# One written order for every operation from the first load to the third MLP round, with each attention period ordered on its own

## The chip, the cores and the metric

The kernel runs on one core of one Trainium2 chip. The metric is the device time of one execution in microseconds; lower is better. A core has a matrix engine (TensorE, PE in the rows; its weight loads are PEld), a vector engine (DVE), a scalar engine (ACT), GpSimd (POOL) and a queue that issues transfers (SP). Each engine works through its own list of instructions in order, and waits on semaphores for the others.

## What is computed

Three layers follow one another (batch 2, 8 heads, 768 positions, head size 64, width 512):

```python
mask = q_bucket[:, :, :, None] == k_bucket[:, :, None, :]     # buckets: signs of q, k times a 64 x 6 projection
scores = np.where(mask, scale * np.matmul(q, k.transpose(0, 1, 3, 2)), -1e9)
attn = softmax(scores); x = attn @ v                           # attention
theta = x @ w_theta                                            # mixing layer
y = w_tok_r @ (x * cos(theta)) + w_tok_i @ (x * sin(theta))
u = x + y; x = u + relu(u @ w_ch)
xn = layernorm(x) * g_ln; out = x + relu(xn @ w_ch1) @ w_ch2   # MLP
```

Every matrix product is done as three products of a high and a low part of its operands, so each operand is split first ("hi", a rounding cast, and "lo", the difference).

## The kernel before

**Attention.** The 16 heads of 768 rows are cut into 48 periods of 256 rows (two tiles of 128). Head h has periods 3h to 3h+2. For period p and tile i the operations, by the names of the order's text, are: `S.p.i` four PE matmuls of the scores into PSUM (`s_mm`, L332), `M.p.i` the row maximum on DVE (L340), `E.p.i` the exponential on ACT (L356), `R2.p` the reciprocal of the row sums on DVE (L363), `tb.p` a small POOL operation (L347), `n.p.i` the normalisation on POOL (L367), `U.p.u` four PE transposes into one PSUM bank (u = 0, 1, 2; L380; `U.p.0` and half of `U.p.1` read `n.p.0`, the rest `n.p.1`), `H.p.u` and `L.p.u` the hi and lo part of the transposed weights on ACT (L389) and DVE (L101), `PV.p` twelve PE matmuls with v (L405), `O.p` on ACT (L414) and `X.p` on DVE (L423), which empty the one PSUM bank of `PV`. So `PV.p+1` cannot start before `X.p`.

**Operands of a head.** The query and key of a head are stacked by six transfers inside SBUF (`sk.h`, L248 to L253) and two small ones for the bucket bits (`sb.h`, L262 and L263). A period's second pair of score matmuls reads the bits. The bits are made from the split q and k by `bits_chunk` on PE, one operation each on ACT (L304) and DVE (L310), and a last one on POOL (`bw`, L666, for pairs 1 to 3; `B1` to `B4` for pairs 4 to 7).

**Side work in the attention.** The weights of theta (eight tiles) are converted while the attention runs: one POOL, one ACT, two DVE operations (`conv_low` L125 and `conv_join` L131), one ACT, one POOL. There are also the splits of v, q and k and the first splits of x (`z_hi`, `z_lo`).

**What sets the order.** The program is emitted operation by operation, and each engine runs its own in that order. Periods 0 to 7 are written out, one token per operation, in a text `head`. From step 8 on a fixed row of tokens with a lag (`plan`) is repeated for each step, and another (`plan_b`) for the four steps that make the bits of the last pairs; the side work hangs on three slots of the plan ("G", "C", "D") by step numbers. The lines that matter:

```python
    plan = (
        ("Sa", 0), ("U0", 2), ("L2", 3), ("nb", 2), ("Ma", 0), ("H0", 2), ("X", 4), ("D", 0),
        ("R2", 1), ("U1", 2), ("Sb", 0), ("Mb", 0), ("H1", 2), ("U2", 2), ("Ea", 0), ("ta", 0), ("H2", 2),
        ("G", 0), ("na", 1), ("PV", 3), ("tb", 0), ("Eb", 0), ("L0", 2), ("C", 0), ("L1", 2), ("O", 3),
    )
```

From the end of the attention on, texts again name every operation: `tail` (the last periods beside the first theta products `z_m`, L790), `half1` (mixing and channel layer), `trans` (the first three MLP rounds). Later MLP rounds follow two fixed texts.

Of the kernel before, what the change touches and what calls it, by code (L numbers as in the profile page):

```python
# [33 lines left out]
def attn_moe_kernel(  # L34
# [398 lines left out]
    def theta_steps(c, x, y):  # L433

        r = slice(256 * x, 256 * x + 256)
        o = {}

        def s():
# [3 lines left out]
            o["t"] = conv_tiles(ap_, th_st[c, x])  # L442
            conv_s(*o["t"])

        return (
            (at, 0, s), (at2, y, lambda: conv_y(*o["t"])), (at3, 1, lambda: conv_low(*o["t"])),
            (at3, 1 + y, lambda: conv_join(*o["t"])), (at2, 1 + y, lambda: cast(act, WA["h"][:, c, r], o["t"][1])),
            (at, 2 + y, lambda: sub(pool, WA["l"][:, c, r], o["t"][1], WA["h"][:, c, r])),
        )
# [104 lines left out]
    TS = tuple(range(22, 46, 3))  # L554
    bg, bg2, bg3 = {}, {}, {}

    def at(step, fn, *args):
        bg.setdefault(step, []).append((fn, args))

    def at2(step, fn, *args):  # L560
        bg2.setdefault(step, []).append((fn, args))

    def at3(step, fn, *args):
        bg3.setdefault(step, []).append((fn, args))


    for h in range(5, B * H):
        at({8: 20}.get(h, 3 * h - 7), stack_dma, h)
        at({8: 21, 9: 21}.get(h, 3 * h - 7), stack_bits, h)
    v_steps = {2: (6, 9, 10), 3: (15, 16, 18), 4: (20, 22, 23)}  # L570
    for n in range(2, NPAIR):
        ld, *hi = v_steps.get(n, (6 * n - 6, 6 * n - 3, 6 * n - 2))
        at(ld, load_v, n)
        for x in range(2):
            at2(hi[x], v_hi, n, act, x)
            at(hi[x] + 1, v_lo, n, pool, x)
    for n, ld in ((6, 8), (7, 13)):
        at(ld, load_raw, n)
    for nm, n, *hi in (
        ("k", 5, 7, 11), ("q", 5, 8, 9), ("k", 6, 12, 13), ("k", 7, 14, 15),  # L580
        ("q", 6, 16, 17), ("q", 7, 17, 18),
    ):
        for x in range(2):
            at2(hi[x], split_hi, nm, n, act, x)
            at(hi[x] + 1, split_lo, nm, n, pool, x)
    for i in range(8):
        c, x = divmod(i, 2)
        at(TS[i] - 2 if i < 2 else max(TS[i] - 3, TS[i - 2] + 2), theta_load, c, x)
        for slot, d, fn in theta_steps(c, x, int(i < 7)):
            slot(TS[i] + d, fn)  # L590
# [18 lines left out]
    for step, fn, j, a in (  # L609
        (30, z_hi, 0, 0), (31, z_hi, 0, 1), (32, z_lo, 0, 0), (32, z_lo, 0, 1),  # L610
        (33, z_hi, 1, 0), (36, z_hi, 1, 1), (37, z_lo, 1, 0), (38, z_lo, 1, 1),
        (38, z_hi, 2, 0), (39, z_hi, 2, 1), (43, z_lo, 2, 0), (44, z_lo, 2, 1),
    ):
        at(step, fn, j, a)
# [3 lines left out]

    def run_bg(q):
        def run(p):  # L620
            for fn, args in q.pop(p, []):
                fn(*args)
        return run

    ops = {
        "Sa": lambda p: s_mm(p, 0), "Sb": lambda p: s_mm(p, 1),
        "Ma": lambda p: s_max(p, 0), "Mb": lambda p: s_max(p, 1),
        "ta": lambda p: None, "tb": s_lone,
        "Ea": lambda p: s_exp(p, 0), "Eb": lambda p: s_exp(p, 1),
        "R2": s_recip, "na": lambda p: s_norm(p, 0), "nb": lambda p: s_norm(p, 1),  # L630
        "B1": lambda p: bits_chunk(*bq[p], "T1"), "B2": lambda p: bits_y_(*bq[p]),
        "B3": lambda p: bits_b_(*bq[p]), "B4": lambda p: bits_p_(*bq[p]),
        "PV": pv_mm, "O": pv_evac_a, "X": pv_evac_b,
    }
    for u in range(3):
        ops[f"U{u}"] = lambda p, u=u: p_transpose(p, u)
        ops[f"H{u}"] = lambda p, u=u: p_hi(p, u)
        ops[f"L{u}"] = lambda p, u=u: p_lo(p, u)
    K0 = 8
    nxt = {op: K0 - d for op, d in plan}  # L640

# [45 lines left out]
    head = """
        sh.k.0.0.0 pb.0.0 pb.0.2 sl.k.0.0.0 pb.0.1 sh.k.0.1.0 sl.k.0.1.0 sh.q.0.0.0 sl.q.0.0.0 sh.q.0.1.0 ac.0
        sl.q.0.1.0 fk ac.1 ay.0 ay.1 kz.1.1 ac.2 ay.2 D.0.0 ab.0 lr.3.0 ab.1 ac.3 sh.k.1.2.0 D.0.1 ay.3 ab.2
        sh.q.1.2.0 aw.0.1 aw.1.1 pb.1.0 aw.2.0 kz.0.0 ab.3 Q.0.0 M.0.0 Q.0.1 warm.17 pb.1.2 E.0.0 lr.3.1 M.0.1  # L690
        sl.q.1.2.1 E.0.1 pb.1.1 D.1.0 sl.k.1.2.0 sh.k.3.2.0 Q.1.0 tb.0 lr.2.0 R2.0 lr.2.1 aw.3.0 M.1.0 n.0.1
        sk.1 sh.k.2.2.0 D.1.1 n.0.0 E.1.0 U.0.2 Q.1.1 U.0.0 sh.q.3.2.0 sl.k.2.2.0 sl.k.3.2.0 U.0.1 sl.q.3.2.1
        H.0.0 D.2.0 M.1.1 H.0.2 bc.0.1 L.0.2 L.0.0 Q.2.0 sh.q.2.2.0 E.1.1 M.2.0 by.0 tb.1 H.0.1 bc.1.0 D.2.1
        lv.0 bb.0 sl.q.2.2.1 L.0.1 by.1 sb.1 R2.1 Q.2.1 bw.0.1 n.1.0 E.2.0 bb.1 vh.0.0 lr.4.0 bc.3.1 M.2.1
        vh.0.1 S.3.0 lr.5.0 vl.0.0.0 bc.2.0 by.3 bw.1.1 E.2.1 U.1.0 by.2 M.3.0 S.3.1 bb.3 n.1.1 U.1.1 E.3.0
        vl.0.1.1 R2.2 bb.2 U.1.2 tb.2 bw.3.1 H.1.0 M.3.1 n.2.0 H.1.1 S.4.0 PV.0 H.1.2 E.3.1 L.1.0 L.1.1 lr.4.1
# [787 lines left out]
```

## Time and profile before

| what | value |
|---|---|
| time, median of 3 runs | 664.09 us (663.68 to 665.66) |
| span of the profiled execution | 662.6 us, 11210 instructions |
| the three runs against that span | 1.0 to 3.0 us above it |
| PE busy | 99% of the span |
| DVE, ACT, POOL busy | 84%, 63%, 47% |
| granted TensorE clock | 1.00 throughout |

The span runs from the first to the last instruction of the profiled execution; the profile does not list that execution's own time, so the runs' distance to the span stands for what lies around it. A busy share of PE does not tell its pace: matmuls overlap, and the record of one ends some 0.16 us after the next could start, so that a short wait of PE shows as a longer step from one start to the next.

### The profile page before, as it was taken

The page shows a single profiled execution, that of the slowest core. Times are in us where ns is not written, and L with a number is a line of the kernel's source. Part 1 is how long each engine was busy: PE and PEld are TensorE (multiplying, and loading weights), DVE is VectorE, ACT ScalarE, POOL GpSimd, SP SyncE. Part 2 cuts the span into 40 slices and gives each one's busy share as a digit, 9 for nine tenths or more (in the row PEclk, how much of TensorE's full clock was granted, in tenths as well). Part 3 has the DMA queues.
Part 4 walks back from the last instruction along what each step waited for, and adds up shares of the span by engine and source line. Part 5 has one row for each costly group of instructions (what it writes and reads, how often), then busy time and mean ns, then how long its engine had stood idle before and what let it go on. Part 6 is the DMA issues. An engine that isn't in the chain of part 4 may idle for free.

```text
span 662.6 us, 11210 instructions
## 1 busy us (share of the span) xinstructions
PE 657.1 (99%) x3771; PEld 591.7 (89%) x3771; DVE 557.5 (84%) x1002; ACT 416.4 (63%) x864; POOL 310.5 (47%) x418
## 2 busy tenths in 40 slices
PE   9999999999999999999999999999999999999998
PEld 7999999999999888888888888989998999999997
...
GB/s 248 240 176 173 135 108 114 116 172 128 127 96 0 161 51 61 80 75 95 148 81 64 48 96 65 63 1 64 64 65 66 62 96 33 97 49 46 1 80 111
DMA packets 32374, 62.24 MB, mean 94 GB/s; under 512 B 4482, under 2 KB 11732, under 8 KB 32317
## 3 DMA queue, kind: packets, MB, share of 16 engines
...
q8 instruction: 30, 0.49, 0.3%
q14 instruction: 27, 0.22, 0.1%
...
## 4 chain that ended last, share of the span: by engine, by line
PE 95%; DVE 2%; DMA 1%; SPq 1%; POOL 1%; issue 0%; ACT 0%; POOLq 0%
PE o L1191 20%; PE acc L856 15%; PE o L405 9%; PE s L332 9%; PE t L380 9%; PE Z L1148 8%; PE a L898 5%; PE v L1148 5%; PE th L790 4%; PE zy L1148 2%; PE Y L1148 2%; PE bits L286 2%; PE s L503 1%; PE xt L967 1%; PE ut L883 1%; DMA tk<-bits 1%
## 5 line engine op out<-in xcount | busy, mean ns | idle before, releaser
L1191 PE MATMUL o<-arena,hh 128*128 128x512 f32 (+1 forms) x388 | 119.1, 388 | 0.0
L367 POOL TENSOR_SCALAR pn<-p,l,M 128x768 f32<-128x768 f32 x96 | 94.6, 986 | 38.8 <-DVE l L363 25.6
L340 DVE TENSOR_REDUCE M<-s 128x1 f32<-128x772 f32 x96 | 90.9, 947 | 4.1 <-PE s L515 2.0
L101 DVE TENSOR_TENSOR ptl<-t,pth 128x512 fp32r<-128x512 f32 x144 | 90.6, 678 | 1.3 <-ACT pth L389 1.0
L356 ACT ACTIVATE p<-s,M 128x772 f32<-128x772 f32 x96 | 87.5, 912 | 2.4 <-DVE M L340 2.0
L117 POOL TENSOR_SCALAR cs<-st 128x512 f32<-128x512 f32 (+2 forms) x68 | 44.8, 665 | 84.6 <-DVE cy L131 75.1
L1191 PEld LDWEIGHTS o<-arena,hh 128*128 128x128 f32 x388 | 72.1, 188 | 13.6
L389 ACT ACTIVATE pth<-t 128x512 fp32r<-128x512 f32 x144 | 81.1, 599 | 4.3 <-PE t L380 3.0
L332 PE MATMUL s<-tk,tq 128*128 128x386 f32 (+1 forms) x360 | 82.8, 351 | 0.0
L380 PE MATMUL t<-ident,pn 128*128 128x128 f32 x576 | 80.3, 273 | 0.4 <-POOL pn L367 0.4
L1191 PE MATMUL o<-arena,hl 128*128 128x512 f32 (+1 forms) x194 | 75.5, 389 | 0.0
L856 PE MATMUL acc<-arena,tokh 128*128 128x512 f32 x240 | 75.3, 395 | 0.0
L380 PEld LDWEIGHTS t<-ident,pn 128*128 128x128 f32 x576 | 68.5, 141 | 6.3 <-POOL pn L367 1.4
L1156 ACT ACTIVATE sn<-Z 128x384 f32<-128x384 f32 x39 | 19.2, 492 | 67.2 <-PE Z L1148 67.2
L332 PEld LDWEIGHTS s<-tk,tq 128*128 128x128 f32 (+1 forms) x360 | 59.4, 190 | 0.1
L856 PEld LDWEIGHTS acc<-arena,tokh 128*128 128x128 f32 x240 | 44.0, 188 | 8.5
L1198 DVE TENSOR_TENSOR U<-o,U 128x512 f32<-128x512 f32 x48 | 32.9, 689 | 21.2 <-PE o L1191 20.5
L856 PE MATMUL acc<-arena,tokl 128*128 128x512 f32 x120 | 46.9, 391 | 0.0
L405 PE MATMUL o<-pth,vv 128*128 128x256 f32 x288 | 46.0, 295 | 0.1
L131 DVE SCALAR_TENSOR_TENSOR cy<-cy,cs 128x512 uint32<-128x512 uint32 (+2 forms) x72 | 41.4, 575 | 3.6
L114 ACT ACTIVATE cy<-st 128x512 f32<-128x512 f32 (+2 forms) x72 | 39.5, 561 | 7.8 <-DVE tokl L101 2.5
L125 DVE SCALAR_TENSOR_TENSOR cs<-st,cs 128x512 uint32<-128x512 uint32 (+2 forms) x76 | 44.1, 580 | 0.2
(260 smaller groups left out, 1481.8 us busy)
## 6 DMA issues: line engine op xcount, KB each, us to landing
...
```

Of the source, the lines that this page charges most:

```text
L101: eng.tensor_tensor(out=o, in0=i, in1=f(hi), op=ALU.subtract)
L117: eng.tensor_scalar(out=s, in0=f(t)[:, :, 1], scalar1=0.0, scalar2=1.0, op0=ALU.mult, op1=ALU.mult)
L332: pe.matmul(ps[:, hf, 0:HW], lt[0:K, x * 128:(x + 1) * 128], rt[0:K, hf, :], start=(K == 128), stop=(K != 128),)
L340: vec.tensor_reduce(out=m_t[p][:, 0, i:i + 1], in_=s_ps[p, i][:, :, 0:HW], axis=AX.XY, op=ALU.max, negate=True)
L356: act.activation(pt, ps[:, :, 0:HW], AF.Exp, bias=m[:, 0, i:i + 1], accum_out=l_t[p][:, 0, i:i + 1])
L367: pool.tensor_scalar(out=pn.rearrange("p (h c) s -> p h (c s)", h=2), in0=p_t.pop((p, i))[:, :, 0:HALF], scalar1=l_t[p][:, 1, i:i + 1], sc ...
L380: pe.transpose(ps[:, w * 128:(w + 1) * 128], pn_t[p, i][:, c, :], ident)
L389: act.activation(ph, t_ps[p, u], AF.Copy)
L405: pe.matmul(ps, vv[:, c, e].rearrange("p a d -> p (a d)"), x[:, c::NI, :], start=(k == 0), stop=(k == 2 * NI - 1),)
L856: pe.matmul(acc, w[:, x, t * 128:(t + 1) * 128], z[:, x, y, :], start=(j == 0 and k == 0), stop=(j == NI - 1 and k == 5),)
L1148: pe.matmul(ps_t[r, b], W1[g][y][:, w, d, :], XB[s][x][:, z, d, :], start=(first == 1 and k == 0), stop=(k == 5), skip_group_check=True,)
L1191: pe.matmul(ps, lt[:, i * 128:(i + 1) * 128], W2[g][:, y, x, n], start=(k == 0), stop=(k == 5))
```

## The change

`plan`, `plan_b` and the slots are removed. `head` now names every operation of all 48 periods and of the side work, in one text; `tail`, `half1` and `trans` are written anew. The 2175 operations are the same ones, with the same engines; only their order differs, and 38 periods from 8 to 45 have 38 different orders. Cut to its core:

```diff
-    plan = (
-        ("Sa", 0), ("U0", 2), ("L2", 3), ("nb", 2), ("Ma", 0), ("H0", 2), ("X", 4), ("D", 0),
...
+    def theta_step(c, x, k):
...
+        elif k == 2:
+            conv_low(*t)
+        elif k == 3:
+            conv_join(*t)
...
     head = """
-        sh.k.0.0.0 pb.0.0 pb.0.2 sl.k.0.0.0 pb.0.1 sh.k.0.1.0 sl.k.0.1.0 sh.q.0.0.0 sl.q.0.0.0 sh.q.0.1.0 ac.0
...
+        sh.k.0.0.0 sh.k.0.1.0 pb.0.0 pb.0.2 sh.q.0.0.0 sh.q.0.1.0 fk sl.k.0.0.0 pb.0.1 sl.k.0.1.0 sl.q.0.0.0 ac.0
...
-    steps = [(k, plan_b if k - 2 in bq else plan) for k in range(K0, NPER)]
...
+    run(head)
```

**Place 1: a middle period on PE and POOL** (the stretch from `S.32.0` to `PV.29`). Names are those above: s is S, t is U, o is PV, pn is n; the first number is the period, the second the tile or the third u. PE before:

```order
L332 MATMUL s32_0_2528<-tk10_2066,tq10_2064 128x386 x2
L332 MATMUL s32_0_2528<-tk210_2067,tq210_2065 128x386 x2
L380 MATMUL t30_0_2533<-ident_62,pn30_0_2505 128x128 x4
L380 MATMUL t30_1_2548<-ident_62,pn30_0_2505 128x128 x2
L380 MATMUL t30_1_2548<-ident_62,pn30_1_2539 128x128 x2
L332 MATMUL s32_1_2553<-tk10_2066,tq10_2064 128x386 x2
L332 MATMUL s32_1_2553<-tk210_2067,tq210_2065 128x386 x2
L380 MATMUL t30_2_2560<-ident_62,pn30_1_2539 128x128 x4
L405 MATMUL o29_2575<-pth29_2465,vv4_2018 128x256 x6
```

PE now:

```order
L332 MATMUL s32_0_2527<-tk10_1960,tq10_1958 128x386 x2
L332 MATMUL s32_0_2527<-tk210_1961,tq210_1959 128x386 x2
L380 MATMUL t30_0_2540<-ident_62,pn30_0_2519 128x128 x4
L380 MATMUL t30_1_2546<-ident_62,pn30_0_2519 128x128 x2
L380 MATMUL t30_1_2546<-ident_62,pn30_1_2497 128x128 x2
L380 MATMUL t30_2_2551<-ident_62,pn30_1_2497 128x128 x4
L332 MATMUL s32_1_2562<-tk10_1960,tq10_1958 128x386 x2
L332 MATMUL s32_1_2562<-tk210_1961,tq210_1959 128x386 x2
L405 MATMUL o29_2583<-pth29_2487,vv4_1853 128x256 x6
```

POOL before, around the two normalisations of period 30:

```order
L367 TENSOR_SCALAR pn30_0_2505<-p30_0_2418,l30_2417,M_66 128x768
L347 TENSOR_SCALAR M_66<-M_66 128x2
L367 TENSOR_SCALAR pn30_1_2539<-p30_1_2444,l30_2417,M_66 128x768
L98 TENSOR_SCALAR xhl0_2571<-xT0_486 128x256
L367 TENSOR_SCALAR pn31_0_2573<-p31_0_2489,l31_2488,M_66 128x768
```

POOL now:

```order
L367 TENSOR_SCALAR pn30_1_2497<-p30_1_2462,l30_2439,M_66 128x768
L367 TENSOR_SCALAR pn30_0_2519<-p30_0_2440,l30_2439,M_66 128x768
L347 TENSOR_SCALAR M_66<-M_66 128x2
L101 TENSOR_TENSOR vv5_2312<-vs5_2125,vv5_2312 128x6x64
L367 TENSOR_SCALAR pn31_1_2581<-p31_1_2537,l31_2523,M_66 128x768
```

`U.30.2` has moved ahead of `S.32.1`. Both normalisations of a period now stand in a row, tile 1 first, and in the whole text both come ahead of the period's `U.p.0`; in the plan `n.p.1` came after `U.p.0`, in the next step.

**Place 2: the theta operations on DVE** (same stretch; cs and cy are the theta tiles, l is R2, xT is X). Before:

```order
L340 TENSOR_REDUCE M_66<-s32_0_2528 128x1
L423 TENSOR_TENSOR xT1_2255<-o28_2507,ot28_2526 64x256
L131 SCALAR_TENSOR_TENSOR cy_2423<-cy_2423,cs_2424 128x256
L363 RECIPROCAL l31_2488<-l31_2488 128x2
L340 TENSOR_REDUCE M_66<-s32_1_2553 128x1
```

Now:

```order
L340 TENSOR_REDUCE M_66<-s32_0_2527 128x1
L423 TENSOR_TENSOR xT1_2279<-o28_2506,ot28_2534 64x256
L125 SCALAR_TENSOR_TENSOR cs_2320<-st_2138,cs_2320 128x256
L363 RECIPROCAL l31_2523<-l31_2523 128x2
L131 SCALAR_TENSOR_TENSOR cy_2319<-cy_2319,cs_2320 128x256
L340 TENSOR_REDUCE M_66<-s32_1_2562 128x1
```

In the plan the sixteen stand always between X and R2, in periods 25, 26, 28, 29, 31, 32, 34, 35, 37, 38, 40, 41, 43, 44 and twice in 46. Now their place and period vary: 23, 25, 26, 29, twice 32, 35, 36, twice 38, 40, 42, 43, 46 and twice 47; in period 32 one stands ahead of R2 and one behind it.

**Place 3: the transfer queue (SP) in the first periods** (tk2h, tq2h: the second operand pair of head h; the rows with bits are `sb.h`). Before:

```order
L253 DMA tk22_518<-lok1_85 64x772
L174 DMA vs1_533<-in_v_dram 128x6x128
L166 DMA raws_76<-in_qT_dram 128x768
L262 DMA tk22_518<-bits_312 7x772
L263 DMA tq22_516<-bits_312 7x2x384
L248 DMA tq4_601<-hiq2_94 64x768
```

Now:

```order
L253 DMA tk24_384<-lok2_93 64x772
L106 DMA st_465<-in_w_theta_dram 128x512
L174 DMA vs1_490<-in_v_dram 128x6x128
L262 DMA tk24_384<-bits_340 7x772
L263 DMA tq24_382<-bits_340 7x2x384
L262 DMA tk22_329<-bits_340 7x772
L263 DMA tq22_327<-bits_340 7x2x384
```

The stack of head 4 and both its bit transfers have moved ahead of the bit transfers of head 2, which period 6 needs first.

## Rows read from the trace of the kernel before

**Rows 1.** The page's first lines: span, then busy time, share, instructions.

```profile
span 662.6 us, 11210 instructions
...
PE   657.1 (99%) x3771; PEld 591.7 (89%) x3771; DVE 557.5 (84%) x1002; ACT 416.4 (63%) x864; POOL 310.5 (47%) x418
```

**Rows 2.** Waits of PE's weight loads, whole span: us in total, times, longest.

```profile
PEld t L380 <- POOL pn L367: 1.4, 5, 0.6
...
PEld o L405 <- DVE xT L423: 0.9, 4, 0.3
PEld xps L773 <- PE xps L773: 0.6, 1, 0.6
PEld zy L1148 <- DVE c L1163: 0.5, 1, 0.5
...
PEld xps L773 <- DVE r L806: 0.3, 1, 0.3
```

**Rows 3.** PV matmuls, stretch 53 to 86 us: count, durations, first and last start.

```profile
L405 PE MATMUL o<-pth,vv x48: 278/282/365, 53.2 to 83.1; 128*128 128x256 f32 x48
```

**Rows 4.** The same, stretch 125 to 224 us.

```profile
L405 PE MATMUL o<-pth,vv x138: 277/282/387, 126.3 to 221.3; 128*128 128x256 f32 x138
```

**Rows 5.** PE in order of time, 156 to 165 us: start, us, instructions merged.

```profile
156.21 0.97 PE L405 MATMUL o<-pth,vv 128*128 128x256 f32 x6
...
160.71 0.97 PE L405 MATMUL o<-pth,vv 128*128 128x256 f32 x6
...
162.94 1.04 PE L380 MATMUL t<-ident,pn 128*128 128x128 f32 x8
```

**Rows 6.** DVE in order of time, same stretch.

```profile
160.23 0.42 DVE L423 TENSOR_TENSOR xT<-o,ot 64x256 f32<-64x256 f32 x1
160.68 0.17 DVE L363 RECIPROCAL l<-l 128x2 f32<-128x2 f32 x1
160.77 0.94 DVE L340 TENSOR_REDUCE M<-s 128x1 f32<-128x772 f32 x1
161.62 1.87 DVE L101 TENSOR_TENSOR ptl<-t,pth 128x512 fp32r<-128x512 f32 x3
163.42 0.95 DVE L340 TENSOR_REDUCE M<-s 128x1 f32<-128x772 f32 x1
164.29 0.40 DVE L423 TENSOR_TENSOR xT<-o,ot 64x256 f32<-64x256 f32 x1
164.62 0.40 DVE L125 SCALAR_TENSOR_TENSOR cs<-st,cs 128x256 uint32<-128x256 uint32 x1
164.95 0.15 DVE L363 RECIPROCAL l<-l 128x2 f32<-128x2 f32 x1
```

**Rows 7.** POOL in order of time, same stretch.

```profile
161.05 0.99 POOL L367 TENSOR_SCALAR pn<-p,l,M 128x768 f32<-128x768 f32 x1 [0.35 <-DVE l L363]
162.12 0.22 POOL L347 TENSOR_SCALAR M<-M 128x2 f32<-128x2 f32 x1
```

**Rows 8.** POOL and DVE in order of time, at 40 us.

```profile
40.02 0.62 POOL L347 TENSOR_SCALAR M<-M 128x2 f32<-128x2 f32 x1
...
40.01 0.54 DVE L221 SCALAR_TENSOR_TENSOR lok<-raws,hik 128x384 fp32r<-128x384 f32 x1
```

**Rows 9.** ACT and PE in order of time, first 9 us.

```profile
4.55 0.52 ACT L210 ACTIVATE hik<-raws 128x384 fp32r<-128x384 f32 x1 [0.65 <-DMA raws<-in_kT_dram]
...
5.37 0.44 PE L286 MATMUL bits<-hik,pb_hi 128*128 128x384 f32 x1
```

**Rows 10.** POOL, SP and PE in order of time, 31 to 37 us.

```profile
31.76 0.66 POOL L666 TENSOR_SCALAR bits<-bb,cst_sb 64x384 fp32r<-64x384 f32 x1
...
32.44 0.84 SPq L263 DMA_DIRECT2D tq<-bits  x1
...
36.50 0.96 PE L332 MATMUL s<-tk,tq 128*128 128x386 f32 x4
```

More of the change, by code (lines that the diff above doesn't have):

```diff
@@ L441, in s @@
                 WA["l"] = const.tile([128, 4, 512], F32R, tag="wAl", name="thl")
[L442 to L449, printed above, removed]
-    order.enter_context(tc.manual_schedule())
-    plan = (
[3 rows of a table removed]
-    )
-    plan_b = (
[4 rows of a table removed]
-    )
+            th_o[c, x] = conv_tiles(ap_, th_st[c, x])
+        t = th_o[c, x]
+        if k == 0:
+            conv_s(*t)
+        elif k == 1:
+            conv_y(*t)
+        elif k == 2:
+            conv_low(*t)
+        elif k == 3:
+            conv_join(*t)
+        elif k == 4:
+            cast(act, WA["h"][:, c, r], t[1])
+        else:
+            sub(pool, WA["l"][:, c, r], t[1], WA["h"][:, c, r])
+    order.enter_context(tc.manual_schedule())
     PH = "kq"
@@ L553, in attn_moe_kernel @@
         pool.memset(f(t[64:128]), 0.0)
[L554 to L590, printed above, removed]
     zx, zq_ = {}, {}
@@ L607, in z_lo @@
         sub(pool, z_slot(j, a, 1), z_src(j, a), z_slot(j, a, 0))
[L609 to L614, printed above, removed]
     bq = {}
@@ L617, in attn_moe_kernel @@
         bq[17 + x] = ([4, 5, 6, 7], PH[x // 2], x % 2)
[L619 to L640, printed above, removed]
     def stk_bits(h):
@@ L654, in g_load, with raw_pair @@
         sp.dma_start(out=gT, in_=g_ln.rearrange("(c p) -> p c", p=128))
+    def raw_pair(n):
+        load_raw(n)
     def kz_copy(y, e):
@@ L690, in attn_moe_kernel @@
[L690 to L694, printed above, removed]
@@ L700, in attn_moe_kernel @@
-        n.4.0 L.3.0 vh.1.0 L.3.2 PV.2 E.5.1 L.3.1 sl.q.4.0.1 U.4.2 O.2 vh.1.1 M.6.0 sk.3 R2.5 X.2 vl.1.0.1
-        U.4.0 sb.3 S.6.1 tb.5 H.4.0 sl.k.4.1.0 sb.4 U.4.1 H.4.2 M.6.1 n.5.0 E.6.0 H.4.1 L.4.0 E.6.1 PV.3 n.5.1
-        S.7.0 U.5.0 sh.q.4.1.0 O.3 L.4.2 L.4.1 M.7.0 H.5.0 U.5.2 S.7.1 X.3 R2.6 tb.6 U.5.1 E.7.0 H.5.1 H.5.2
-        M.7.1 PV.4 vl.1.1.1 L.5.0 sl.q.4.1.1 n.6.0 E.7.1 tb.7 O.4 L.5.1
-    """
-    for w in head.split():
-        op, *args = w.split(".")
-        hops[op](*(int(x) if x.isdigit() else x for x in args))
@@ L710, in attn_moe_kernel @@
-    steps = [(k, plan_b if k - 2 in bq else plan) for k in range(K0, NPER)]
-    for k, now in steps:
-        for op, d in now:
-            if op == "G":
-                run_bg(bg)(k - 2)
-            elif op == "C":
-                run_bg(bg2)(k - 2)
-            elif op == "D":
-                run_bg(bg3)(k - 2)
-            elif op[0] == "B":
-                ops[op](k - 2)
-            else:
-                while nxt[op] <= min(k - d, NPER - 1):
-                    ops[op](nxt[op])
-                    nxt[op] += 1
+        sh.k.0.0.0 sh.k.0.1.0 pb.0.0 pb.0.2 sh.q.0.0.0 sh.q.0.1.0 fk sl.k.0.0.0 pb.0.1 sl.k.0.1.0 sl.q.0.0.0 ac.0
@@ L727, in attn_moe_kernel, with run @@
+        tq.3.1.5 O.44 E.47.1 tb.47
+    """
+    def run(text, **names):
+        for w in text.format(**names).split():
+            op, *args = w.split(".")
+            ops[op](*(int(x) if x.isdigit() else x for x in args))
+    run(head)
     bctx.close()
@@ L1333, in attn_moe_kernel @@
+        xb_l.0.1.4.1 madd.1.0.1 xb_h.0.1.5 ch_at.6 cv_h.e.1 xb_l.0.1.5.0 mix.35.0 cv_y.e.2 cv_l.e.1.1 madd.1.1.1
+        ch_ah.6 ch_al.6 mix.35.1 cv_b.e.2 xb_l.0.1.3.0 ch_at.9 cv_h.e.2 xb_h.0.1.2 cv_l.e.2.1 xb_l.0.1.2.0
     """
@@ L1377, in attn_moe_kernel @@
+        xb_h.1.1.3 xb_l.1.1.4.1 o_mm.1.3 h_hi.2.11 xb_l.1.1.3.0 xb_h.1.1.5 xb_l.1.1.5.1 prod.2.5 o_add.1.3 prod.2.7
+        o_mm.1.5 snap.2.3 h_add.2.22 h_lo.2.11 h_hi.2.22 prod.2.4 h_lo.2.22 o_add.1.5 prod.2.3 h_hi.2.21 h_lo.2.21
+        o_add.1.4
     """
```

325 lines of the change are left out of this document (166 added, 159 removed), and 6 rows, old and new, of tables (plan, plan_b).

## The prediction

> **What bounds the kernel now.** I read the page first. PE is busy 657.1 us of a span of 662.6 [rows 1], so no other engine's total can set the end; but the busy share hides short waits, since the record of a matmul reaches past the start of the next. The second view is therefore the table of waits for PE's weight loads [rows 2], where a late operand shows, and the third the pace of PE: how far the starts of the same block lie apart.
>
> The waits first. Away from the start, five groups are worth naming: the transposes waited five times for the normalisation on POOL (1.4 us, the longest 0.6), PV four times for X on DVE, which empties its one bank (0.9), and the transposes of x and a product of the MLP waited 0.6, 0.3 and 0.5 [rows 2]. The first two lie in the part that the repeated plan orders (from 53 us on); the last three, 1.4 us together, lie in `tail` and `trans`, where every operation already had a written place.
>
> The pace second. From 53 to 86 us there are 48 PV matmuls with the hi part, six for each period, so eight periods; the sixth of a block starts 0.69 us after the first (the six last 0.97 [rows 5], one lasts 0.28 [rows 3]). The first starts at 53.2, the last at 83.1, so seven steps are 29.9 - 0.69 = 29.2 us and a period is 4.17 us [rows 3]. No PE wait of the table falls in them, so 4.17 is what PE's own work takes. From 126.3 to 221.3 there are 138, hence 23 blocks and 22 steps: (95.0 - 0.69) / 22 = 4.286 us [rows 4]. Where the theta weights are converted, a period is thus 0.115 us longer, together 2.5 us. With the single wait of 0.6 us, which lies between the two stretches, the plan's part loses **3.1 us**. All that the change could remove is these 3.1 and the 1.4 of the texts: 4.5 us of 662.6.
>
> Why theta costs there: DVE. One period of it, from R2 to R2, is 160.68 to 164.95 [rows 6]: R2 0.09, M 0.85, three L 1.80, M 0.87, X 0.33, the theta operation 0.33. Without theta that is 3.94 us of the 4.17 that PE needs, so 0.23 us are left in a period, less than one theta operation. The plan puts 16 of them into 22 periods: 16 x 0.33 / 22 = 0.24 us a period against 0.23. DVE falls behind and X comes late: at 160.71 PV starts as X, begun at 160.23 and 0.42 long, ends, and it comes 4.50 us after the PV before it (156.21) instead of 4.17 [rows 5, 6].
>
> **The change, part by part.**
> - *Work.* The operations and their engines are the same. A gain can come only from waits of PE.
> - *Theta on DVE (place 2).* 14 of the 16 operations now lie in the 24 periods from 23 to 46, that is 14 x 0.33 / 24 = 0.19 us a period, below the 0.23; two moved into the last period, beside the theta products. The load alone no longer forces a wait. But they still come in twos (32 and 38 have two each), so some of them should still reach PE: two in one period make DVE 0.66 - 0.23 = 0.43 us late. Bounds for what remains of the plan's 3.1 us: below, nothing, as in the periods up to 53 us, which were written out singly and have the same operations and none of these waits; above, the density of the other written texts, 1.4 us in about 260 us (24 to 53 us and 220 to 450), times the 168 us from 53 to 221: 0.9 us. I take 0.5: the work is that of the former, but DVE is as full as nowhere in it. **Gain 3.1 - 0.5 = 2.6 us.** The wait of 0.6 for POOL was one long hold-up in one period, and goes with the plan.
> - *PE's order within a period (place 1).* `U.p.2` ahead of `S.p+2.1` issues the same matmuls; PE's pace by itself does not change. It gives H.2 and L.2 more time before PV. Counted as nothing; what covers it is that the four score matmuls that moved behind are needed by M, and DVE is busy with three L by then.
> - *Both normalisations ahead of `U.p.0`.* A deadline that comes earlier for the second of them; its price is a rival below. In the sum: nothing.
> - *Tail, half1, trans.* Rewritten, as they were written before: the same density of waits, so 1.4 us before and 1.4 us now. The ends are 0 and twice as much.
> - *The first microseconds.* ACT now splits the second half of k, which waits for its transfer until 4.55 and takes 0.52 [rows 9], ahead of the two casts of the projection. These end at about 5.4 instead of before 4, and the difference made from them on DVE at about 5.6; the first bits matmul started at 5.37 [rows 9]. The four bits products now stand together, ahead of both score groups, so part of the delay may be won back. Bounds 0 and 0.4 us; I take **a loss of 0.2**.
> - *SP (place 3).* Head 2's bits are now issued behind the stack of head 4, a theta tile, v and head 4's bits. The last q bits on POOL ended at 32.42 and the transfer that reads them was issued at 32.44 for 0.84; `S.6.0` started at 36.50 [rows 10]. In the new POOL order some 1.6 us of other work stands ahead of the last bits, so about 34.0, then three small transfers at 0.84 each: issued by 36.5. `S.6.0` itself now stands behind `PV.2` and starts 1.4 us later, about 38, its second pair 0.36 after. The cover is the landing time of the last transfer, which no row gives; if it takes 2 us the operand is just in time. Bounds 0 and 0.5; I take 0.
>
> Sum: -2.6 + 0.2 = -2.4 us. Against the span this is 662.6 - 2.4 = 660.2; against the median of the runs, 664.09 - 2.4 = **661.7 us**, since the runs lie 1.0 to 3.0 above the span and nothing outside the span changes.
>
> **A rule weighed.** The small POOL operation M took 0.62 us where it ran beside a DVE operation that reads two SBUF operands, and 0.22 us in a stretch without one [rows 7, 8]. The Trainium skill, "GPSIMD Engine Reference", § 8 Key points, says that GpSimd shares its SBUF interfaces with VectorE and contends with its instructions in a 2-port mode or with two SBUF inputs; by this rule the trace agrees, with the 0.40 us. The theta operations read two SBUF operands. In the plan they stood ahead of R2, and the normalisation waits for R2, so they never ran beside it; in the new order four of them (periods 32, 36, 38 and 43) stand right behind R2 and run beside `n`. If each holds it up by 0.40 us and nothing absorbs it, 1.6 us come back: 663.3 us. That is the first rival.
>
> **Rivals.**
> - *Contention of theta and n*: 661.7 + 1.6 = 663.3, by the paragraph above. Against it: four places of forty periods, and `n` has some slack where R2 is early. Chance 0.10.
> - *The waits only move.* The theta operations stay in the same stretch and in twos, DVE keeps over 95% of PE's period, and the written texts themselves have 1.4 us of waits, so a written order is no proof of none. If the plan's 3.1 us stay, the start takes its 0.2: 664.3. Chance 0.16.
> - *All of it goes*: 664.09 - 4.5 = 659.6. For it: the load on DVE falls below the limit, and the periods up to 53 us show that such an order can run without waits. Against: two of the three written texts have some. Chance 0.19.
> - *Slower: the second normalisation comes too late for `U.p.0`.* In a period delayed by theta R2 starts at 160.68, `n` at 161.05, and it lasts 0.99 [rows 6, 7]; the next transposes start at 162.94 [rows 5], with one `n` done and the second needed only later. Now both must be done: 0.37 + 2 x 0.98 + about 0.1 to hand over = 2.43 us after R2, and there are 162.94 - 160.68 = 2.26. If R2 stays that late in all 40 periods, each waits 0.17 us: 6.8 us lost, while the old 3.1 us go (the waiting gives DVE its time): 664.09 + 3.7 = 667.8. It decides at R2 later than 2.43 us before the transposes. Against it: where DVE is not behind, R2 is up to 0.23 us earlier, and in several of the new periods R2 stands ahead of X or of M. Chance 0.13.
>
> **How the numbers follow.** The forecast has 0.42, with a spread of its own from 660.4 (nothing left at the plan, no loss at the start, 0.6 less in the texts) to 662.8 (0.9 left, 0.4 and 0.5 lost at the start and the bits). About 0.3%, 2.0 us, is what a measurement of this kernel tells from no change, so faster means below 662.1 and slower above 666.1. Of the forecast 0.30 lies below 662.1 and 0.12 above. Faster: 0.30 + 0.19 = 0.49. Same: 0.12 + 0.10 + 0.16 = 0.38. Slower: 0.13. The range from 659.4 to 664.8 holds all but the slow case and a little of the edges.
>
> **What would show it.** Right: PV starts 4.17 to 4.2 us apart from 126 to 221 us where they were 4.286, X and `pn` gone or below 0.6 us together in the table of waits, the first bits matmul at 5.4 to 5.8. Wrong: waits of transposes for `pn` spread over many periods (the slow rival), POOL's `pn` longer beside theta (contention), the score matmuls of period 6 waiting for their bits, or new waits after 220 us above 1.4.

## The result: slower by 0.9%

| | before | after |
|---|---|---|
| time, median | 664.4 us (663.5 to 665.9, 6 runs) | 670.7 us (668.8 to 673.5, 6 runs) |
| ratio | 1 | 1.0094, 95% interval 1.0073 to 1.0115 |
| span of the profiled execution | 662.6 us | 670.1 us |

The kernel is 6.3 us slower where 2.4 us less were forecast; the range ended at 664.8. The profiled execution took 671.84 us, 1.8 above its span. Three of the six runs have a granted clock of 0.999 or 1.000 and take 668.8 to 669.9 us, the other three 0.995 to 0.997 and 671.6 to 673.5; the profiled one is among the latter. The page of the profile after, first lines and the row of the clock:

```profile
span 670.1 us, 11172 instructions
...
PE 661.1 (99%) x3771; PEld 594.0 (89%) x3771; DVE 559.9 (84%) x1002; ACT 414.2 (62%) x864; POOL 310.5 (46%) x418
...
PEclk8999999999999999999999998999999999999999
```

Busy times answer to [rows 1] within a few us: the work is the same, and 7.5 us of span have come from waits, or from work at a lower clock (the two 8s of the last row). The waits of PE's weight loads over the whole span, those that answer to [rows 2] and the new ones:

```profile
PEld zy L1130 <- DVE c L1145: 2.3, 1, 2.3
PEld t L380 <- POOL pn L367: 2.2, 7, 0.5
...
PEld bits L286 <- PE warm L540: 1.2, 1, 1.2
PEld xt L949 <- POOL xn L939: 0.8, 2, 0.4
PEld t L380 <- PE t L380: 0.8, 1, 0.8
...
PEld s L506 <- POOL hik L203: 0.6, 1, 0.6
...
PEld o L405 <- DVE xT L423: 0.6, 3, 0.2
```

The waits for `pn` and X, which the forecast wanted gone, are 2.8 us where they were 2.3. New are one of 2.3 us in `trans`, two of 0.4 at `xn` near the end of `trans`, one of 0.8 in the attention and those at the start. The clock, in the two stretches where it was not full (columns: stretch, length, then busy time of PE, PEld, DVE, ACT and POOL with their instructions, granted clock, DMA share, GB/s):

```profile
10.00:12.00 2.00, 1.72 (x9) 1.47 (x9) 1.31 (x3) 1.80 (x5) 1.54 (x5) 0.78 0.85 263
12.00:14.00 2.00, 2.00 (x11) 2.00 (x10) 2.00 (x3) 1.98 (x5) 1.91 (x3) 0.50 0.85 246
...
402.30:405.00 2.70, 2.58 (x12) 2.45 (x13) 1.96 (x4) 0.39 (x1) 0.55 (x1) 0.75 0.52 159
405.00:408.00 3.00, 3.00 (x10) 2.35 (x10) 1.89 (x3) 0.20 (x1) 2.29 (x4) 0.66 0.44 143
```

0.50 is the lower of TensorE's two levels, 1.2 GHz. There the 17 transposes of `warm` start 213 ns apart instead of 109, 1.7 us in all, and the matmuls from 402.4 to 407 us lose another 1.7 by their steps. The steps sort the loss by place. PV.n is the first of a block of twelve PV matmuls, counted from 0 (all 576 are in each of these traces):

| profiled execution, us | before | after |
|---|---|---|
| start of PV.0 | 28.8 | 31.1 |
| PV.0 to PV.47 | 212.6 | 213.3 |
| of it PV.8 to PV.43 | 154.55 | 155.54 |
| PV.47 to the end | 421.2 | 425.6 |

So 2.3 us at the start, 0.7 in the attention and 4.4 behind it. PV.8 to PV.43 is the part whose orders were the point of the change, and it became 1.0 us longer. From PV.20 on, where the theta operations stand, it became 1.5 us longer (99.67 against 98.13). Ahead of PV.20 it became 0.6 shorter, nearly all by one period of the old order, PV.14, which took 4.88 us there and 4.09 now.

### The profile page after: what moved, and what is told of

Same layout as the page of the kernel before. It is cut to its first block, busy times and chain, and to the rows that moved or that the text cites. A ratio compares the mean times of both kernels' runs of the same rounds, so it can differ in the third digit from the quotient of the medians.

```text
span 670.1 us, 11172 instructions
## 1 busy us (share of the span) xinstructions
PE 661.1 (99%) x3771; PEld 594.0 (89%) x3771; DVE 559.9 (84%) x1002; ACT 414.2 (62%) x864; POOL 310.5 (46%) x418
## 4 chain that ended last, share of the span: by engine, by line
PE 83%; DVE 9%; DMA 2%; issue 2%; ACT 1%; POOL 1%; SPq 0%; POOLq 0%; DVEq 0%; ACTq 0%
PE o L1173 19%; PE acc L838 14%; PE Z L1130 8%; PE o L405 8%; PE s L332 7%; PE t L380 7%; PE th L772 5%; PE v L1130 5%; PE a L880 4%; DVE ptl L101 3%; DVE M L340 3%; PE Y L1130 2%; DMA raws<-in_kT_dram 2%; PE bits L286 1%; PE zy L1130 1%
## 5 line engine op out<-in xcount | busy, mean ns | idle before, releaser
L1173 PE MATMUL o<-arena,hh 128*128 128x512 f32 (+1 forms) x388 | 119.2, 389 | 0.0
L101 DVE TENSOR_TENSOR ptl<-t,pth 128x512 fp32r<-128x512 f32 x144 | 93.3, 678 | 3.3 <-ACT pth L389 2.9
L1173 PEld LDWEIGHTS o<-arena,hh 128*128 128x128 f32 x388 | 72.1, 188 | 13.8
L389 ACT ACTIVATE pth<-t 128x512 fp32r<-128x512 f32 x144 | 79.6, 598 | 3.1 <-PE t L380 2.7
L380 PE MATMUL t<-ident,pn 128*128 128x128 f32 x576 | 75.1, 274 | 0.8 <-DVE ptl L101 0.6
L1173 PE MATMUL o<-arena,hl 128*128 128x512 f32 (+1 forms) x194 | 75.5, 389 | 0.0
L380 PEld LDWEIGHTS t<-ident,pn 128*128 128x128 f32 x576 | 65.8, 141 | 6.6 <-POOL pn L367 2.2
L1180 DVE TENSOR_TENSOR U<-o,U 128x512 f32<-128x512 f32 x48 | 33.1, 690 | 21.1 <-PE o L1173 20.3
L131 DVE SCALAR_TENSOR_TENSOR cy<-cy,cs 128x512 uint32<-128x512 uint32 (+2 forms) x72 | 43.6, 605 | 5.7 <-ACT cy L114 2.6
L405 PE MATMUL o<-pth,vv 128*128 128x256 f32 x288 | 44.3, 289 | 0.0
```

The lines of the kernel that those rows point to most:

```text
L101: eng.tensor_tensor(out=o, in0=i, in1=f(hi), op=ALU.subtract)
L380: pe.transpose(ps[:, w * 128:(w + 1) * 128], pn_t[p, i][:, c, :], ident)
L389: act.activation(ph, t_ps[p, u], AF.Copy)
L405: pe.matmul(ps, vv[:, c, e].rearrange("p a d -> p (a d)"), x[:, c::NI, :], start=(k == 0), stop=(k == 2 * NI - 1),)
L1173: pe.matmul(ps, lt[:, i * 128:(i + 1) * 128], W2[g][:, y, x, n], start=(k == 0), stop=(k == 5))
```

## Experiments

All orders are edits of the written text; the kernels of one section compare with the kernel before by ratios, since groups of runs differ by up to 0.7 us in its median.

### trans: one pair in the wrong order, and what it cost

VectorE in order of time in the changed kernel, then PE and GpSimd there:

```profile
396.31 0.69 DVE L885 SCALAR_TENSOR_TENSOR U<-a,U 128x512 f32<-128x512 f32 x1 [0.24 <-PE a L880]
399.82 0.69 DVE L125 SCALAR_TENSOR_TENSOR cs<-st,cs 128x512 uint32<-128x512 uint32 x1 [2.82 <-POOL cs L117]
400.61 0.69 DVE L131 SCALAR_TENSOR_TENSOR cy<-cy,cs 128x512 uint32<-128x512 uint32 x1
401.22 0.68 DVE L101 TENSOR_TENSOR uxl<-ut,uxh 128x512 fp32r<-128x512 f32 x1
401.82 0.55 DVE L1145 TENSOR_TENSOR c<-zy,sn 128x384 f32<-128x384 f32 x1
...
402.42 0.62 PE L1130 MATMUL zy<-arena,w1h 128*128 128x384 f32 x2 [1.91 <-DVE c L1145]
...
394.11 0.74 POOL L101 TENSOR_TENSOR arena<-cy,arena 128x256 fp32r<-128x256 f32 x1 [2.20 <-ACT arena L94]
394.83 0.96 POOL L117 TENSOR_SCALAR cs<-st 128x512 f32<-128x512 f32 x1
399.12 0.66 POOL L117 TENSOR_SCALAR cs<-st 128x512 f32<-128x512 f32 x1 [3.34 <-DMA st<-in_w_dram]
```

PE stood 2.07 us for `c` (the 1.91 of the row and the 0.16 by which a record reaches past the next start), but `c` took 0.55 us; what was late is two places ahead of it in VectorE's queue, `cv_b.v.1.0` on a weight tile. Its load could not go out before the subtraction at 394.11 gave its memory free, since SyncE's queue waited for that:

```profile
SPq L1006 <- POOL arena L101: 21.1, 1, 21.1
```

The other tile of the pair, v.1.1, had its load issued at 372.9. On VectorE (`cv_b`) the new order converts v.1.0 first; the old one v.1.1.

```diff
-... ch_al.9 cv_y.v.1.0 prod.0.2 cv_s.v.1.0.1 ch_br.6 cv_b.v.1.0 ch_at.7 ch_bm.9 ch_ah.7 cv_y.v.1.1 ... ch_br.9 cv_b.v.1.1
+... ch_al.9 cv_y.v.1.1 prod.0.2 cv_s.v.1.0.1 ch_br.6 cv_b.v.1.1 ch_at.7 ch_bm.9 ch_ah.7 cv_y.v.1.0 ... ch_br.9 cv_b.v.1.0
```

**trans_swap** is the changed kernel with this exchange.

> The changed kernel with one pair exchanged: in the text trans the converted tile v.1.1 (whose load went out at 372.9 us) takes the early place of cv_y and cv_b, and v.1.0 (loaded only at 394.9 us) the late one, as in the order before. Theory: the 2.07 us wait of zy at 400 us stands there because VectorE's two operations on the late tile are queued ahead of the sum c of the round, and the matmuls from 402.4 to 407 us at half clock (1.7 us over their nominal spacing, added up) follow from that wait; both go together: 3.8 us, from 670.7 to 666.9 us (666.0 to 667.8). Rival A: the late load only moves its wait to a later matmul; 669.5 us or more. Rival B: the wait goes but the lower clock comes all the same, from another cause; 668.6 us.

668.84 us (667.85 to 672.61); ratio 1.0076 (1.0053 to 1.0098). In the profile PV.47 to the end fell from 425.6 to 421.7, by 3.9 us where 3.8 were expected; the wait is gone and the clock full. The median fell by 1.9 us only and lies above the range that was expected. The start, the same text, was different again in this run (below), which hides the size. So the pair was measured once more, behind the start of the old kernel: **trans_price** is start_before (below) without the exchange.

> start_before with the change's own trans, v.1.0 ahead of v.1.1 again: the start of the kernel before takes the start's spread out, so that the price of this one pair is seen by itself (between the changed kernel and trans_swap the medians gave 1.9 us, the profiled runs 3.9 us from PV.47 to the end). Theory: the wait of 2.07 us and 1.7 us of half clock behind it, 3.8 us more than start_before: 670.0 us (669.2 to 670.8), PV.47 to the end 425.6 us. Rival A: the clock does not fall in most runs, and the pair costs the wait alone: 668.3 us. Rival B: with the earlier start the load lands before it is asked for, and the wait is smaller than 1 us: 667 us or less.

668.98 us (668.20 to 669.79); ratio 1.0080 (1.0066 to 1.0094), against 1.0032 of start_before: the pair costs 0.0048, 3.2 us, between the theory (3.8) and rival A (the wait alone). The profiled run takes 424.2 us from PV.47 to the end, 2.4 more than start_before. PE in order of time, and the stretches behind (columns as above):

```profile
400.54 0.62 PE L1130 MATMUL zy<-arena,w1h 128*128 128x384 f32 x2 [2.28 <-DVE c L1145]
```

```profile
400.60:404.00 3.40, 3.40 (x19) 3.02 (x20) 2.82 (x5) 0.60 (x1) 1.36 (x2) 1.00 0.58 192
404.00:408.00 4.00, 4.00 (x22) 3.50 (x21) 3.61 (x9) 2.48 (x6) 1.51 (x3) 1.00 0.12 47
```

The wait, 2.44 us by the steps of PE, is longer than in the changed kernel, and the clock behind it stays full. Rival A holds for this profiled run. Three profiles have the pair: the wait stands in all of them, the lower clock behind it in two (start_pb has granted clocks of 0.83 and 0.60 there).

### The start: which loads go first

**start_pb** takes up the one thing that the prediction priced there, the casts of the projection behind the second half of k.

```diff
-sh.k.0.0.0 sh.k.0.1.0 pb.0.0 pb.0.2 sh.q.0.0.0 sh.q.0.1.0 fk sl.k.0.0.0 pb.0.1 sl.k.0.1.0
+sh.k.0.0.0 pb.0.0 pb.0.2 sh.k.0.1.0 sh.q.0.0.0 sh.q.0.1.0 pb.0.1 fk sl.k.0.0.0 sl.k.0.1.0
```

> The changed kernel with the three casts and subtractions of pb moved up in the first line of head, ahead of the second half of hik (the place that they have in the order before). Theory: the first bits matmul then waits 0.5 us less, and the 17 transposes of warm, which ran at 213 instead of 109 ns beginning 6 us after that wait (1.7 us in all), run at full clock because TensorE no longer stands 1.1 us between the first warm matmuls and the bits: 670.7 to 668.5 us (668.0 to 669.2). Rival A: the clock falls for the wait of 0.43 us at 9.9 us, which stays; then only 0.5 us are gained, 670.2 us. Rival B: the loads of heads 1 to 3 set the start whatever the casts do, and nothing is gained; 670.7 us.

671.83 us (670.07 to 676.24); ratio 1.0118 (1.0092 to 1.0144): nothing gained, as rival B had it. The kernel **both** has start_pb's and trans_swap's edits.

> The two edits before this one together. If the loss stands in these two places with their two stretches of half clock, they add up: 670.7 - 3.8 - 2.2 = 664.7 us (663.8 to 665.6), level with the kernel before. If the loss lies spread over the attention's own orders, most of it stays: 668 us or more.

668.72 us (667.35 to 671.91); ratio 1.0071 (1.0050 to 1.0093): no better than trans_swap. My theory of the start failed in both, and their profiles say why. ScalarE and PE of start_pb, then PE of both, where each stood longest at the start:

```profile
18.32 0.84 ACT L210 ACTIVATE hik<-raws 128x768 fp32r<-128x768 f32 x1 [1.94 <-DMA raws<-in_kT_dram]
...
20.84 0.63 PE L494 MATMUL s<-tkz,hiq 128*128 128x386 f32 x2 [2.76 <-ACT p L356]
```

```profile
41.94 0.60 PE L332 MATMUL s<-tk,tq 71*128 71x386 f32 x2 [2.01 <-DMA tk<-bits]
```

In start_pb the k of head 3 landed at 18.3 us, `sh.k.3.2.0` waited for it on ScalarE, and the exponentials that free the score bank were queued behind. In the kernel both, and in trans_swap too (1.3 us), `S.6.0` waited for its bits. The wait of 1.06 us at the first bits matmul (by the steps of PE), which I had taken for the cause, was 0.29 us in trans_swap with the same text. The waits of this start differ from run to run.

**start_before** takes the whole start back: the order of before up to PV.8, then the change's, with the exchange in `trans`.

> The order of the kernel before up to PV.8, from there the change's own order, with the exchange of v.1.0 and v.1.1 in trans as in trans_swap. No seam at the tail, unlike attn_only. Theory: the start's loads were the larger and more variable part of the loss (stalls of 0.9 to 3.0 us at 18 to 21 us and of 1.5 to 2.2 us at 39 us in the three profiles with the change's start); with the start of before only the attention's orders (PV.8 to PV.43 1.0 us longer, PV.0 to PV.47 0.7 us longer) and the late xn at 436 us (0.8 us) are left: 664.3 + 0.7 + 0.6 = 665.6 us (664.9 to 666.6). Rival: the change's order after PV.8 has waits for loads of its own that the late start only hid: 667.5 us or more.

666.22 us (665.52 to 671.60, 12 runs); ratio 1.0032 (1.0017 to 1.0047), as expected. PV.0 is at 29.4 us; in the profiles of the six kernels here that have the old order up to PV.8 it lies between 29.2 and 30.0, so that one profile prices a start to no better than 0.8 us. Against trans_swap the start costs 0.0044, 2.9 us, and eleven of the twelve runs lie within 1.5 us.

What in it? SyncE's queue at the start, after, shows that q of head 3 was put first, waits for its buffer until 7.2 us, and k stands behind it and behind lv.0 (`vs`):

```profile
7.21 0.33 SPq L166 DMA_DIRECT2D raws<-in_qT_dram  x1
7.58 0.43 SPq L166 DMA_DIRECT2D raw<-in_kT_dram  x1
8.05 0.54 SPq L174 DMA_DIRECT2D vs<-in_v_dram  x1
8.63 0.54 SPq L166 DMA_DIRECT2D raws<-in_kT_dram  x1
```

Before, k went out at 5.7 us and `vs` at 14.1. **loads** gives trans_swap the old order of these five loads:

```diff
-lr.3.1 ... lr.2.0 ... lv.0 ... lr.3.0 ... lr.2.1 ... sk.1 ... vh.0.0 ... vh.0.1
+lr.3.0 ... lr.3.1 ... lr.2.0 ... lr.2.1 ... sk.1 lv.0 ... vh.0.0 vh.0.1
```

> trans_swap with the loads of the start in the order before: the two halves of head 3's raw tile first, then head 2's, and lv.0 behind sk.1 (vh.0.0 moves behind it). Theory: in the change q of head 3 stands first in SyncE's queue and waits for loq until 7.2 us, so k goes out at 8.63 instead of 5.70 us and lands at 17 to 18.3 us, and TensorE stalls 0.9 to 3.0 us at 18 to 21 us; in the order before that stall is gone: 668.8 to 667.3 us (666.4 to 668.2), with the wait for the bits of S.6.0 at 39 us left where it occurs. Rival: the transfers themselves are slow there, in whatever order; 668.8 us.

669.48 us (669.22 to 670.02); ratio 1.0073 (1.0060 to 1.0086): no gain. In the profile the stall at 18 to 21 us is gone, but PE waits 1.13 and 0.68 us for VectorE's bits at 26 and 32 us, and the transposes of `warm` run at the lower clock again (granted 0.84, 0.50 and 0.81 from 10 to 16 us). Put back alone, among the change's orders of the other engines, the old loads gain nothing. **loads_back** asks the other way: start_vl (below), which has the old start, with only these five loads in the change's order.

> start_vl, that is the start in the order of the kernel before, with only the loads of the first heads in the change's order: q of head 3 first, one half of head 2, lv.0, then k of head 3 and the other half of head 2, all ahead of sk.1; the orders of the other engines stay. Theory: the late k of head 3 is what costs the start: the stalls at 14 to 21 us come back, 1 to 3 us more than start_vl, 666.4 to 668.4 us, with more spread from run to run. Rival (for which the run with the loads put back spoke): the order of the casts and subtractions on ScalarE, VectorE and GpSimd makes the loss, not the loads: 665.4 us, within 0.4 us of start_vl.

667.27 us (664.93 to 668.25); ratio 1.0038 (1.0025 to 1.0052) against 1.0015 of start_vl. The loads alone cost 0.0023, 1.5 us (by the two intervals 0.0007 to 0.0039), with a spread of 3.3 us over seven runs where start_vl has 2.0 over eleven. The profiled run was one without a stall (span 663.8), so no trace shows the stall behind this loss. The order of the loads costs something, then, even among the old orders of the other engines; its share of the start's loss in the changed kernel was not taken apart.

### The attention: theta on VectorE, and a collision

**attn_only** puts the change's orders from PV.8 on into the old kernel, with the old tail, half1 and trans.

> The order of the kernel before up to PV.8, then the change's order of everything that is left of head, then tail, half1 and trans of the kernel before without what is already done: the change's own orders of the periods 8 to 45 alone. The prediction's term for them was a gain of 2.5 us: 661.9 us. Theory now: VectorE is busy 97 to 98 of 99 us there in both kernels, so no order can take the waits away; the stretch from the first to the last PV was 213.3 us against 212.7 us: 0 to 1 us slower than before, 664.4 to 665.4 us. Rival: the order gains and the changed kernel only hid it behind its late start: 663.0 us or less.

668.23 us (667.37 to 668.34); ratio 1.0053 (1.0040 to 1.0065). PV.8 to PV.43 is 155.57 us, as after, but two waits of 0.9 and 1.1 us at 224 and 244 us stand at the seam to the old tail, and PV.0 stands 1.1 us later than before, at 30.0. The expected time was missed, and the time as a whole is not a price of the attention. The stretch is: 155.47 to 155.81 in all eight kernels that have the change's orders there unedited, 154.55 before, for the same 1152 matmuls of PE.

The largest single piece of it is one period, that of PV.34 (5.18 us against 4.18 before). VectorE, GpSimd and PE, after:

```profile
181.31 0.68 DVE L101 TENSOR_TENSOR ptl<-t,pth 128x512 fp32r<-128x512 f32 x1
181.91 1.23 DVE L125 SCALAR_TENSOR_TENSOR cs<-st,cs 128x256 uint32<-128x256 uint32 x1
183.06 0.68 DVE L101 TENSOR_TENSOR ptl<-t,pth 128x512 fp32r<-128x512 f32 x1
...
181.85 1.00 POOL L101 TENSOR_TENSOR vv<-vs,vv 128x384 fp32r<-128x384 f32 x1
...
183.88 0.63 PE L380 MATMUL t<-ident,pn 128*128 128x128 f32 x4 [0.61 <-DVE ptl L101]
```

The theta operation `cs` takes 0.40 us in [rows 6] and 1.23 here. GpSimd's subtraction began 0.06 us before it, and `cs` ended 0.28 us after the subtraction: it stood for as long as the other ran. Two more theta operations of this trace show the same: one of 0.66 us at 169.57 behind a subtraction that ended at 169.95, one of 0.78 at 224.85 behind one that ended at 225.35; both end 0.28 us after it. In the old order none from PV.8 to PV.43 took over 0.43 us. The Trainium skill, "SBUF — State Buffer", section "SBUF: two separate sides", states that a VectorE operation with two SBUF inputs and a GpSimd operation that reads SBUF exclude each other for a whole instruction, and that the one that starts first goes on; these rows agree. **start_vl** is start_before with one operation moved:

```diff
-vh.6.1 S.38.0 tq.2.0.2 O.34 vl.6.1.1 E.37.1 L.35.2 U.36.0 U.36.1 M.38.0 tq.2.1.0 U.36.2
+vh.6.1 S.38.0 tq.2.0.2 O.34 E.37.1 L.35.2 U.36.0 U.36.1 M.38.0 tq.2.1.0 vl.6.1.1 U.36.2
```

> start_before with one operation moved: GpSimd's two-input subtraction vl.6.1.1 behind tq.2.1.0 in head, so that it no longer begins 0.06 us before VectorE's bit operation on the theta tile, which took 1.23 us there and takes 0.42 us elsewhere. Theory: that operation stood until GpSimd's was over, and the wait of 0.78 us that TensorE has behind it in the period of PV.34 (5.18 us against 4.3) goes: 0.8 us less than start_before, about 664.8 us, and PV.28 to PV.36 in 34.9 us instead of 35.65. Rival A: VectorE is full, and the time comes back within the next two periods: PV.28 to PV.36 stays within 0.2 us. Rival B: the long operation comes from something else and stays at 1.2 us.

665.36 us (664.75 to 666.70); ratio 1.0015 (1.0006 to 1.0024). By the ratios this is 0.0017 or 1.1 us less than start_before, by the medians 0.9, with an interval of 0.0017 on either side; in the profile PV.28 to PV.36 is 35.03 instead of 35.64, as expected, where the old order has 34.26. `cs` there:

```profile
179.74 0.63 DVE L125 SCALAR_TENSOR_TENSOR cs<-st,cs 128x256 uint32<-128x256 uint32 x1
...
179.68 0.41 POOL L117 TENSOR_SCALAR cs<-st 128x256 f32<-128x256 f32 x1
180.06 1.17 POOL L101 TENSOR_TENSOR vv<-vs,vv 128x384 fp32r<-128x384 f32 x1
180.08 1.67 PE L380 MATMUL t<-ident,pn 128*128 128x128 f32 x12
```

`cs` now meets a shorter GpSimd operation, the cast of another theta tile, which began 0.06 us before it and ended at 180.09; `cs` again ends 0.28 us after that, at 0.63 us in all. The subtraction that follows takes 1.17 us instead of 1.00, and the twelve transposes go through without a break. **mended** moves three more.

```diff
-H.24.2 tq.0.1.2 sk.11 U.24.1 R2.25
+H.24.2 R2.25 tq.0.1.2 sk.11 U.24.1
...
-R2.29 X.26 H.28.1 zh.0.1 tl.1.1 U.28.2 n.29.1 M.30.1 E.30.0 sb.11 PV.27 L.28.1 n.29.0
+R2.29 X.26 H.28.1 tl.1.1 U.28.2 n.29.1 M.30.1 E.30.0 sb.11 PV.27 L.28.1 n.29.0 zh.0.1
...
-xn.1.1.0.0 xb_h.1.0.3 xb_l.1.0.4.0 h_hi.1.11 o_mm.0.3 xb_l.1.0.3.1 h_add.1.22 cv_h.w.1.1 o_add.0.2 h_hi.1.22 xn.1.1.1.1
+xn.1.1.0.0 xn.1.1.1.1 xb_h.1.0.3 xb_l.1.0.4.0 h_hi.1.11 o_mm.0.3 xb_l.1.0.3.1 h_add.1.22 cv_h.w.1.1 o_add.0.2 h_hi.1.22
```

> start_vl with three more operations moved. (1) R2.25 ahead of tq.0.1.2: VectorE's reciprocal no longer waits behind a bit operation of 0.42 us, and TensorE's 0.32 us before the transposes of that period (132 us) go. (2) zh.0.1 behind n.29.0: GpSimd's cast of 0.41 us no longer stands ahead of the two normalisations, and the 0.2 us at 149 us go. (3) xn.1.1.1.1 ahead of xb_l.1.0.3.1: GpSimd, idle for 3.7 us before it, makes the xn in time, and the 0.77 us at 430 us go. All three: 1.2 us less than start_vl, 665.4 to 664.2 us, level with or 0.4 us below the kernel before. Rival A: VectorE is the second full engine, so (1) only moves its wait, and GpSimd's (2) likewise: only (3) counts, 664.7 us. Rival B: in (3) the wait moves to the next transposes: 665.2 us.

664.80 us (664.42 to 666.25); ratio 1.0013 (1.0004 to 1.0022). The number is rival A's, but against the kernel before the gain over start_vl is 0.0002, and the profile does not bear rival A out. The wait for `xn` is gone, yet PV.47 to the end is 421.97 us after 421.78: the next products wait three times for VectorE, 1.0 us in the table of weight loads (`PEld o L1173 <- DVE U L1180`). PV.8 to PV.43 fell only from 154.96 to 154.82. So most of what the three moves gave came back at later places. This is the best version found with the new orders, and it does not beat the kernel before.

Is it the order at all? **no_theta_after** (start_before) and **no_theta_before** leave VectorE's 16 bit operations on the theta tiles out; their theta weights are then wrong.

```diff
-        elif k == 2:
-            conv_low(*t)
-        elif k == 3:
-            conv_join(*t)
+        elif k in (2, 3):
+            pass
```

> start_before with VectorE's two bit operations on each theta tile left out (16 operations in all, 5 to 7 us of VectorE between 85 and 220 us; the theta weights are then wrong). Theory: VectorE is the second full engine of these periods (97 to 98 of 99 us), and TensorE's waits there are its queue: with the operations gone PV.8 to PV.43 falls from 155.5 to 153.2 us or less. Rival: the waits come from the order of GpSimd's normalisations, and stay: 154.8 us or more.

> The kernel before with VectorE's two bit operations on each theta tile left out, as in no_theta_after (the theta weights are then wrong). If VectorE's load makes the waits of these periods whatever the order, the kernel before gains as no_theta_after did (2.0 us from PV.8 to PV.43 against start_before, 1.4 us against start_vl): 154.55 to 153.0 us or so (152.7 to 153.4). If the old plan's fixed place for these operations cost TensorE nothing and its waits came from the plan, PV.8 to PV.43 stays above 154.0 us.

| PV.8 to PV.43, us (in brackets PV.20 to PV.43) | all work | without theta's bits | difference |
|---|---|---|---|
| orders of the kernel before | 154.55 (98.13) | 151.91 (96.19) | 2.64 (1.94) |
| orders of the change (start_before) | 155.54 (99.62) | 153.52 (97.61) | 2.02 (2.01) |
| the same, collision mended (start_vl) | 154.96 (99.01) | | |

The time, one run of each without them: 661.7 us for the kernel before (664.2 with them, median), 664.9 for start_before (666.2). 153.52 lies a little above the 153.2 that were expected at most, 151.91 below the 152.7. In the table of waits of no_theta_before no wait of PE is left between 53 and 222 us.

Not all of the 2.64 is theta's. 0.70 of it is the period PV.14 (4.88 us, then 4.18), where the first of these operations was still some 35 us away. In the kernel before a small GpSimd operation waited there for a transfer, with the normalisations queued behind it:

```profile
85.98 0.10 POOL L203 MEMSET lok<- 128x4 f32 x1 [0.94 <-DMA tk<-lok]
```

In no_theta_before, with the same order, that wait is missing. The theta operations of the old order cost 1.9 us. VectorE over one stretch of 99 us, in the changed kernel, and in the kernel before without the 16 operations:

```profile
125.00:224.00 99.00, 98.15 (x731) 92.85 (x730) 97.44 (x174) 92.08 (x201) 69.34 (x100) 1.00 0.41 97
```

```profile
122.00:221.00 99.00, 99.00 (x756) 96.61 (x755) 95.94 (x167) 96.46 (x215) 74.94 (x108) 1.00 0.44 108
```

VectorE (third busy figure) is at 97.44 and 95.94 us, and at 98.22 in the kernel before over the same stretch as the second. This share does not tell where PE waits: from 53 to 86 us the kernel before has VectorE at 98% as well, without a theta operation and without a wait of PE:

```profile
53.00:86.00 33.00, 33.00 (x255) 32.44 (x254) 32.29 (x56) 32.60 (x73) 27.23 (x42) 1.00 0.62 151
```

5.3 us of operations taken out gave 1.9 us. The change's order did not remove the waits that they cause: they cost 2.0 us in it, 0.6 of that in the collision. It also stays 1.6 us longer than the old order without theta (153.52 against 151.91, and 211.41 against 209.78 from PV.0 to PV.47), with waits for `pn` (0.5), the exponential (0.5) and X (0.4): these are the order's own. Whether another order could do without both was not tried.

## Why the prediction was wrong

- **Theta on DVE, gain 2.6: failed; PV.8 to PV.43 became 1.0 us longer instead.** The cause of the 2.5 us was right: without the theta operations the old order is 1.9 us shorter there. The 0.6 for POOL was a wait behind a transfer, which is gone in the new orders but was also missing once in the old one (no_theta_before). The step that failed is the sentence that 0.19 us a period lie below the 0.23 that are free, so that the load alone no longer forces a wait: in the new order the operations still cost 2.0 us, 1.4 without the collision. An average load does not decide it, and the steps of PV in the kernel before had shown this. There each pair of theta operations has three periods. The pairs that start at 139, 165 and 190 us cost PE nothing (steps of 4.17 to 4.20 us), those at 152, 177 and 203 us about 0.5 us each (4.38, then 4.48 to 4.50; 0.1 of it stays without them). What else stands in a period counts; beside the latter GpSimd subtracts a half of v, but that this makes the difference was not tested.
- **The bound for what remains, from the other written texts (0 to 0.9): failed.** Measured from the old orders without theta, 151.91 us, the changed kernel's lose 3.6 us. The density of waits in one text is no property of written texts.
- **Tail, half1, trans: 1.4 before and after, ends 0 and 2.8: failed, and above its end.** PV.47 to the end became 4.4 us longer. One pair in `trans` cost 3.2 us (2.4 to 3.9 in profiles); the waits for `xn` are 0.8. An equal density of waits was assumed, without a look at the loads: I had looked at SP's loads only at the places named, and not at which of two tiles has its load out first.
- **The first microseconds, loss 0.2 (0 to 0.4): mis-sized by four to fourteen times.** The first bits matmul came at 5.92 us, past the 5.8 named as a sign, but in trans_swap, with the same text, at 5.45; putting the casts of the projection back gained nothing (start_pb). The start cost 2.3 us in the profile and 0.9 to 2.9 by the ratios. The reversed loads of heads 2 and 3, 1.5 us behind the old start, stood in the diff and were not priced.
- **SP, `S.6.0`, 0 to 0.5: too low.** No wait in the changed kernel's profile, but 1.3 and 2.0 us in two of the three others with this start. The landing of 2 us, set as a condition without a row, was the weak link: in the kernel both the k bits issued at 36.2 us landed only at 41.6, 5.3 us later.
- **Rivals.** Contention came the other way round: not `n` held up by theta (`pn` took 0.98 to 1.04 us all through) but theta by GpSimd, for 0.8 us at its worst place. "The waits only move" (664.3) comes nearest for the attention, where the waits stayed; that mended (664.8) ends near its number is luck, since the start, `trans` and the tail are mended in it too. The slow rival's number, 667.8, was the nearest to the result, but not for its reason: waits for `pn` are seven, not spread over 40 periods.

By the ratios of the runs, the loss of 0.0094 divides into about 0.003 for the pair in `trans`, 0.003 for the start, 0.0017 for the collision and 0.0015 for the rest. The first two are means: the pair cost 0.0048 behind the old start and 0.0018 behind the new one, the start 0.0044 and 0.0014, and the intervals of these ratios are 0.0014 to 0.0022 on either side, so no part is known to better than about 0.002.
